# Retention attention and a maxout FFN: two neighbouring weight pieces in one load, and one exponent step moved

## The chip, the cores and the metric

The kernel runs on one core of one Trainium2 chip. Times are device microseconds (us) of one execution, as the median of several runs; a profile is one execution more, recorded by the hardware. The core has five engines that run side by side, each with a queue of its own that is worked off in order: TensorE (PE in the profile, its weight loads PEld), VectorE (DVE), ScalarE (ACT), GpSimd (POOL) and SyncE (SP), which here issues loads and stores. A "q" behind an engine's name means its sequencer, so SPq lines are DMA issues.

## The reference

The program has two parts. The first is causal retention over 8 batches, 8 heads, 576 positions and 64 dimensions a head; the second a maxout feed-forward network over the 4608 rows that come out of it.

```python
scores = scale * np.matmul(q, k.transpose(0, 1, 3, 2))
Dmat = np.where(rel >= 0, gamma[:, None, None] ** rel[None, :, :], 0.0)
attn = np.matmul(scores * Dmat[None, :, :, :], v)          # (B, H, S, D)
x = attn.transpose(0, 2, 1, 3).reshape(B * S, H * D)       # (4608, 512)
h = np.maximum(np.maximum(x @ w1, x @ w2), x @ w3)         # (4608, 768)
return h @ w_out                                           # (4608, 512)
```

The four weights arrive as float64: w1, w2 and w3 are 512 x 768, w_out is 768 x 512.

## The kernel before

**Blocks and tiles.** The 4608 rows are cut into 36 blocks of 128 positions (C), four of which make a tile of 512 (NT). A block's q, k and v are loaded (line 259), q and k are transposed on PE (line 295) and copied out of PSUM by ScalarE into kT and qT (line 296), the scores are taken (line 309), masked by VectorE into st (line 221), and multiplied with v (line 464); what comes from older positions is carried in a state (products at line 423, its use at line 479). The result goes to xT, the FFN's input, with the dimension on the partitions. The FFN's up products of the first tile are at line 934, those of the later tiles at line 909.

**The weights.** They are turned into float32 on the chip, from the bits of the float64. `pieces` lists them in the order of use: for each pair of 128-column blocks of the hidden dimension, and for each of w1, w2, w3, two pieces of 128 columns (512 x 128 numbers, 512 KB as float64); then six pieces of w_out. `load_weights(n)` (lines 596 to 610) takes the next n pieces. Two neighbouring pieces share a tile of the tag "bits". A piece of w1, w2 or w3 is loaded by two DMAs of 256 KB, one for each half of the 128 partitions, because the heads are kept in another order on the partitions; every run in HBM is 128 numbers of 8 bytes, 1 KB. A piece of w_out is one DMA of 512 KB with runs of 4 KB.

**The conversion.** The class `Two` has the steps for a pair of pieces: `exponent` (two ScalarE operations, lines 778 and 779), `fraction` (ScalarE at 785 and 788, VectorE at 786), `whole` (VectorE, 791), `sign` (VectorE, 795), `product` (VectorE, 803), which writes the float32 weights and calls `load_weights(1)` for each piece done. The generator `convert_all` goes through the first three pairs piece by piece and through the others pair by pair; every `yield` in it ends one part, and `convert(n)` runs the next n parts. For the first piece the parts are: exponent, fraction, whole, sign with product; the second piece's follow in the same way.

**The order.** Nothing is scheduled by a planner: the order of the program text is the order in every engine's queue. Lines 1059 to 1107 write out the start by hand: which loads stand in which order on SP's queue, which block's transposes, scores, state and values follow on PE, and where `convert` puts the weights' steps between them. After them the loop over tiles calls `ffn(t)` and the attention of the following tile in turns. Blocks 0 to 3 make the first tile; block CPT - 1 is block 3. `first_ups` starts the up products with the first two pieces of w1, on the columns of blocks 0 to 2, before block 3 is finished.

The lines that the change moves are, in the part before the loop:

```python
    load(2, "kq")
    load_weights(1)
    load(2, "v")
    load(CPT - 1, "kq")
    load_weights(1)
    load(CPT - 1, "v")
    load_weights(2)
    load_weights(2)
    decay(0)
```

`decay(0)` multiplies block 0's v by the keys' decay (line 270; on GpSimd for blocks 0 to 2, on VectorE for block 3).

Of the kernel before, what the change touches and what calls it, by code (L numbers as in the profile page):

```python
# [40 lines left out]
FP32 = mybir.dt.float32  # L41
BF16 = mybir.dt.bfloat16
I32 = mybir.dt.int32
U32 = mybir.dt.uint32
I64 = mybir.dt.int64
AF = mybir.ActivationFunctionType
# [53 lines left out]
def kernel(  # L100
# [14 lines left out]
    nc = tc.nc  # L115
# [30 lines left out]
    def half(j):  # L146
        return slice(D * j, D * (j + 1))
# [97 lines left out]
    def load(g, names="kqv"):  # L245
        if g >= BY_PE and "q" in names and ("q", g) not in raws:
            load_blocks(g, *range(C // 32))
        for n, src in (("k", k), ("q", q), ("v", v)) if g < BY_PE else (("k", k), ("v", v)):
            if n not in names:
                continue  # L250
            bufs = {"k": 3, "q": 2, "v": 4}[n]
            pool, bufs = (raw0, 1) if n != "v" and g < BY_PE and g % (bufs + 1) == bufs else (raw, bufs)
            if n == "v":
                t = vpool.tile([C, H, D], FP32, tag="v", name="vraw")
            else:
                t = pool.tile([C, H, D], FP32, tag=n, name=n + "raw", bufs=bufs)
            raws[n, g] = t
            for row, b, pos, m in spans(g):
                nc.sync.dma_start(t[row:row + m], src[b, :, pos:pos + m, :].rearrange("h p d -> p h d"))  # L259
# [15 lines left out]
    def transposes(g, names="kq"):  # L275
        both = qks.setdefault(g, {})
        if both:
            pass
        elif g >= BY_CHUNKS:
            for n, tag in (("k", "kT"), ("q", "m1")):  # L280
                both[n] = att.tile([P, H, D], FP32, tag=tag, name=n + "T", bufs=2 if n == "k" else 3)
        else:
            both["k"] = att.tile([P, NP, C], FP32, tag="kT", name="kT", bufs=2)
            both["q"] = ppool.tile([P, NP, C], FP32, tag="part", name="qT")
        if g >= BY_PE:
            for n in ("k", "q"):
                soon(partial(nc.vector.transpose, both[n][:].rearrange("a p c -> a (p c)"),
                             raws.pop(("kx" if n == "k" else n, g))[:].rearrange("a x y i -> a (x y i)")))
            return
        for n in names:  # L290
            src = raws["k", g] if n == "k" else raws.pop(("q", g))
            pool, tag = (ps_r, "r") if g >= CPT else (ps_x, "x")
            pt = pool.tile([P, NP, C], FP32, tag=tag, name=n + "t")
            for p in range(NP):
                nc.tensor.transpose(pt[:, p, :], pair(src, p), ident[:C, :C])
            nc.scalar.copy(both[n][:], pt[:])
# [145 lines left out]
    def head(c, n):  # L442

        return NP * c + n
# [151 lines left out]
    def load_weights(n):  # L596
        for _ in range(n):
            if not to_load:
                return
            i, fb = piece = to_load.popleft()  # L600
            if fb % 2 == 0:
                bits[i, fb // 2] = wraw.tile([P, 2, DM], I64, tag="bits", name="bits")
            t = bits[i, fb // 2][:, fb % 2, :]
            if i == "out":
                nc.sync.dma_start(t, moe_w_out[fb * P:(fb + 1) * P, :])
            else:
                heads = WS[i][:, fb * P:(fb + 1) * P].rearrange("(h p) f -> p h f", p=D)
                blocks = t.rearrange("p (n f) -> p n f", f=P)
                for c in range(2):
                    nc.sync.dma_start(blocks[half(c)], heads[:, head(c, 0):head(c, NP)])  # L610

    def seven_forms(order):

# [148 lines left out]
    def convert_all():  # L762

        class Two:
            def __init__(self, n):
                self.i, fb = pieces[2 * n]
                self.fp = fb // 2
                words = bits.pop((self.i, self.fp))[:].rearrange("p e f -> p (e f)")  # L770
                self.high = words.bitcast(I32).rearrange("p (e f two) -> p e f two", e=2, two=2)[:, :, :, 1]
                self.top = words.bitcast(BF16).rearrange("p (e f four) -> p e f four", e=2, four=4)[:, :, :, 3]
                self.low = words.bitcast(U32).rearrange("p (e f two) -> p e f two", e=2, two=2)[:, :, :, 0]
                self.expo = wtmp.tile([P, 2, DM], I32, tag="expo", name="expo")
                self.mant = wtmp.tile([P, 2, DM], FP32, tag="mant", name="mant")

            def exponent(self, e):
                nc.scalar.activation(self.expo[:, e, :].bitcast(FP32), self.top[:, e, :], AF.Abs)
                nc.scalar.activation(self.mant[:, e, :], self.low[:, e, :], AF.Identity, bias=one[:], scale=2.0 ** -52)

            def fraction(self, e):
                expo = self.expo[:, e, :]
                if e != TWO[1]:
                    self.frac = wtmp.tile([P, 2, DM], I32, tag="frac", name="frac", bufs=1)
                nc.scalar.activation(expo, expo, AF.Relu, bias=top[:], scale=-2.0 ** -20)
                nc.vector.tensor_scalar(out=self.frac[:, e, :], in0=self.high[:, e, :], scalar1=0xFFFFF, scalar2=None,
                                        op0=ALU.bitwise_and)
                nc.scalar.activation(expo, expo, AF.Relu, bias=inf[:], scale=-2.0 ** 23)

            def whole(self, e):  # L790
                nc.vector.scalar_tensor_tensor(out=self.mant[:, e, :], in0=self.frac[:, e, :], scalar=2.0 ** -20,
                                               in1=self.mant[:, e, :], op0=ALU.mult, op1=ALU.add)

            def sign(self, e):
                nc.vector.scalar_tensor_tensor(out=self.expo[:, e, :], in0=self.high[:, e, :], scalar=-2 ** 31,
                                               in1=self.expo[:, e, :], op0=ALU.bitwise_and, op1=ALU.bitwise_or)

            def product(self, e):
                if self.i == "out":
                    w = w_out[:, self.fp]  # L800
                else:
                    w = w_up[self.i][:, 2 * self.fp:2 * self.fp + 2, :]
                nc.vector.tensor_tensor(w[:, e, :], self.mant[:, e, :], self.expo[:, e, :].bitcast(FP32), op=ALU.mult)
                for n in range(2)[e]:
                    w_sb[self.i, 2 * self.fp + n] = w[:, n, :]
                    load_weights(1)

        TWO = [slice(0, 1), slice(1, 2)]
        both = slice(0, 2)
        two = Two(0)  # L810
        for e in TWO:
            for step in (two.exponent, two.fraction, two.whole):
                step(e)
                yield
            two.sign(e)
            two.product(e)
            yield
        for n in (1, 2):
            two = Two(n)
            for e in TWO:  # L820
                for step in (two.exponent, two.fraction):
                    step(e)
                    yield
            for e in TWO:
                two.whole(e)
                yield
                two.sign(e)
                two.product(e)
                yield
        two = Two(3)  # L830
        two.exponent(both)
        yield
        two.fraction(both)
        two.whole(both)
        yield
        for n in range(4, len(pieces) // 2 + 1):
            following = Two(n) if n < len(pieces) // 2 else None
            if following:
                following.exponent(both)
            two.sign(both)  # L840
            yield
            two.product(both)
            yield
            if following:
                following.fraction(both)
                yield
                following.whole(both)
                yield
            two = following
# [28 lines left out]
    def convert(n):  # L878
        for _ in range(n):
            next(converting, None)  # L880
# [179 lines left out]
    load(0)  # L1060
    load(1)
    load(2, "kq")
    load_weights(1)
    load(2, "v")
    load(CPT - 1, "kq")
    load_weights(1)
    load(CPT - 1, "v")
    load_weights(2)
    load_weights(2)
    decay(0)  # L1070
# [28 lines left out]
    scores(2)  # L1099
    convert(2)  # L1100
    transposes(CPT - 1, "k")
    state(2)
    values([2], [2], middle=[partial(transposes, CPT - 1, "q")])
    keep(2)
    convert(2)
    scores(CPT - 1)
    decay(CPT - 1)

# [98 lines left out]
```

## Time and profile before

| | |
|---|---|
| median of 3 runs | 738.89 us (738.87 to 738.95) |
| the profiled execution | 738.46 us |
| its span, first to last instruction | 736.7 us |
| PE busy | 731.4 us |
| VectorE busy | 572.3 us |
| ScalarE busy | 354.6 us |
| GpSimd busy | 39.1 us |
| loads of w1, w2, w3 | 36, of 256 KB, 6.2 us to landing (median) |
| loads of w_out | 6, of 512 KB, 5.7 us to landing |
| read from HBM, written | 48.80 MB, 9.44 MB |

The profiled execution is one run by itself; a sum of durations from its rows is made against its own 738.46 us, of which 736.7 are the span. A row of a timeline has the start and the time it took in us, engine, line, operation, out<-in by the program's names, how many, and in brackets the idle time of the engine just before and what ended it. A row of the chain of waits has start, us, and what was last to end there. Matmul times overlap, since matmuls are pipelined; the spacing of their starts tells more than one's own duration. DMA issues have their own rows on SP; the landing is the issue's start and the time to landing.

### The profile page before, as it was taken

What the parts mean: (1) busy time and instruction counts of PE and PEld (TensorE: products, weight loads), DVE (VectorE), ACT (ScalarE), POOL (GpSimd) and SP (SyncE); (2) the same over time, 40 slices, a digit from 0 to 9 for tenths busy, and PEclk for the clock granted to TensorE, in tenths of its full rate; (3) what the DMA queues carried; (4) which work ended last, traced back from release to release, by engine and by line L of the source; (5) the groups of instructions that cost most, each with busy time, mean ns of one, the idle gap of its engine ahead of it and who ended that gap; (6) DMA issues with size and microseconds to landing.
All of it is one profiled execution on the core that took longest, in us unless ns stands there. A gap on an engine that the chain in (4) does not pass through costs nothing.

```text
span 736.7 us, 17316 instructions
## 1 busy us (share of the span) xinstructions
PE 731.4 (99%) x6932; PEld 604.1 (82%) x6932; DVE 572.3 (78%) x1051; ACT 354.6 (48%) x740; POOL 39.1 (5%) x44
## 2 busy tenths in 40 slices
PE   9999999999999999999999999999999999999998
PEld 7654457888888888888888888888888888888887
DVE  5998799999886995689668866887768866893676
ACT  4886915444345525543364425543555245424441
POOL 2000010132000100010000000000100010000000
PEclk9999999999999999999999999999999999999999
DMA  9999554314251415151424243322514150000001
GB/s 222 264 233 247 107 98 115 67 27 91 73 100 27 91 42 105 37 97 32 103 52 79 45 109 60 64 53 64 109 29 88 46 125 6 1 31 28 1 1 57
DMA packets 233264, 59.38 MB, mean 81 GB/s; under 512 B 214496, under 2 KB 231904, under 8 KB 233184
## 3 DMA queue, kind: packets, MB, share of 16 engines
q1 hardware_dynamic: 232208, 58.24, 36.5%
q8 instruction: 54, 0.88, 0.5%
q14 instruction: 26, 0.21, 0.1%
q10 hardware_dynamic: 976, 0.04, 0.1%
HBM read 48.80 MB, written 9.44 MB: 79 GB/s over the span
## 4 chain that ended last, share of the span: by engine, by line
PE 97%; SPq 1%; DMA 1%; issue 0%; ACT 0%; DVE 0%
PE a L909 20%; PE b L909 17%; PE c L909 9%; PE up L934 9%; PE di L755 7%; PE d L909 6%; PE e L909 6%; PE dhc L755 5%; PE deg L755 3%; PE sk L377 3%; PE down L921 3%; PE o L528 2%; PE o L535 2%; PE dfd L755 2%; PE dx L662 1%; SPq L259 1%
## 5 line engine op out<-in xcount | busy, mean ns | idle before, releaser
L897 DVE TENSOR_TENSOR part<-part 128x512 f32<-128x512 f32 x168 | 117.9, 702 | 86.5 <-ACT part L894 83.9
L894 ACT COPY part<-b 128x512 f32<-128x512 f32 x120 | 70.3, 586 | 163.3 <-PE b L909 161.6
L897 DVE TENSOR_TENSOR h<-h,part 128x512 f32<-128x512 f32 x120 | 83.3, 694 | 24.0 <-ACT h L894 20.0
L894 ACT COPY part<-a 128x512 f32<-128x512 f32 x96 | 56.3, 586 | 51.6 <-PE a L909 51.1
L209 ACT ACTIVATE vraw<-vraw,gk 128x64 f32<-128x64 f32 x240 | 76.9, 347 | 6.6 <-DMA vraw<-in_v_dram 6.6
L909 PE MATMUL b<-s,n 128*128 128x256 f32 x288 | 73.9, 379 | 0.0
L934 PE MATMUL up<-xT,w 128*128 128x512 f32 (+2 forms) x160 | 63.5, 553 | 0.0
L909 PEld LDWEIGHTS b<-s,n 128*128 128x128 f32 x288 | 54.7, 190 | 7.4
L394 POOL TENSOR_TENSOR s<-s,gs_of 64x512 f32<-64x512 f32 x23 | 25.0, 1089 | 553.6 <-DVE s L392 476.5
L934 PEld LDWEIGHTS up<-xT,w 128*128 128x128 f32 x160 | 28.6, 190 | 30.1 <-issue 27.0
L909 PE MATMUL c<-xT,w 128*128 128x256 f32 x192 | 51.3, 389 | 0.0
L744 ACT COPY k<-di 128x256 f32<-128x256 f32 x49 | 18.3, 373 | 68.5 <-PE di L755 43.4
L909 PE MATMUL d<-s,w 128*128 128x256 f32 x192 | 49.8, 380 | 0.0
L909 PE MATMUL b<-xT,n 128*128 128x256 f32 x192 | 49.3, 379 | 0.0
L909 PE MATMUL a<-s,w 128*128 128x256 f32 x192 | 49.3, 379 | 0.0
L909 PE MATMUL a<-xT,w 128*128 128x256 f32 x192 | 49.3, 379 | 0.0
L909 PE MATMUL e<-xT,w 128*128 128x256 f32 x192 | 45.4, 379 | 0.0
L909 PE MATMUL a<-xT,n 128*128 128x256 f32 x192 | 45.4, 379 | 0.0
L909 PEld LDWEIGHTS e<-xT,w 128*128 128x128 f32 x192 | 36.5, 190 | 5.4 <-issue 0.5
L909 PEld LDWEIGHTS b<-xT,n 128*128 128x128 f32 x192 | 36.5, 190 | 5.0
L909 PEld LDWEIGHTS a<-s,w 128*128 128x128 f32 x192 | 36.5, 190 | 5.0
L909 PEld LDWEIGHTS a<-xT,w 128*128 128x128 f32 x192 | 36.5, 190 | 5.0
(196 smaller groups left out, 1382.1 us busy)
## 6 DMA issues: line engine op xcount, KB each, us to landing
bits<-in_moe_w_dram SPq DMA_DIRECT2D x36, 256.0 KB, 6.2
kraw<-in_k_dram SPq DMA_DIRECT2D x32, 256.0 KB, 3.1
vraw<-in_v_dram SPq DMA_DIRECT2D x32, 256.0 KB, 3.6
qraw<-in_q_dram SPq DMA_DIRECT2D x240, 32.0 KB, 2.1
kxraw<-in_k_dram SPq DMA_DIRECT2D x240, 32.0 KB, 2.1
out_dram<-osb SPq DMA_DIRECT2D x56, 128.0 KB, 1.7
bits<-in_moe_w_out_dram SPq DMA_DIRECT2D x6, 512.0 KB, 5.7
out_dram<-osb SPq DMA_DIRECT2D x7, 256.0 KB, 2.0
```

The lines of the kernel that those rows point to most:

```text
L209: scaling.popleft()()
L377: nc.tensor.matmul(s[half(c), h, :], lhsT=kT[half(c), h, :], rhs=qT[half(c), h, :], start=True, stop=True)
L394: nc.gpsimd.tensor_tensor(new, new, factor, op=ALU.mult)
L528: nc.tensor.matmul(o[m][half(c), n, u, :], lhsT=vds[g][half(m), h, :], rhs=sts[g][half(m), h, :], start=n == 0 and u == 0, stop=place(g, m ...
L535: nc.tensor.matmul(o[m][half(c), n, u, :], lhsT=stacks[g][half(m), h, :], rhs=qks[g]["q"][half(m), h, :], start=False, stop=True, skip_gro ...
L744: nc.scalar.copy(place, a)
L755: nc.tensor.matmul(banks[chain], lhsT=hidden(h, order, b, late_ones)[:, e], rhs=late["V"][v][:, e], start=begins and e == 0, stop=chain no ...
L894: nc.scalar.copy(of[step], ps[step[0]][:])
L897: nc.vector.tensor_tensor(of[dst], a, b, op=op)
L909: nc.tensor.matmul(ps[chain][:, e, :], lhsT=factor(w, 2 * fp + e), rhs=xS[t][x], start=n == 1 and e == 0, stop=ends, skip_group_check=True)
L921: nc.tensor.matmul(b[:], lhsT=h[:, fb, m * P:(m + 1) * P], rhs=w_sb["out", fb], start=fb == blocks[0], stop=fb == blocks[-1])
L934: nc.tensor.matmul(ps[:, a:b], lhsT=w_sb[i, fb][:, dc * P:(dc + 1) * P], rhs=xT[t][:, dc, a:b], start=dc == 0 and a == 0, stop=dc == NDC - ...
```

## The change

Three things are done together.

- `load_weights` loads the two neighbouring pieces of w1, w2 or w3 with the first of them: two DMAs of 512 KB, one for each half of the partitions, with runs of 256 numbers, 2 KB. The call for the second piece of the pair does nothing. w_out is loaded as before.
- In the tiles of the bits and of what is worked out from them, the two pieces now lie interleaved, as the load brings them: four blocks of 256 columns, in each the 128 of the first piece and the 128 of the second. `of(e, ...)` picks one piece's part where a step works on one alone. `product` writes the float32 weights in their old place.
- At the start, both pieces of w1's first pair are loaded where the first piece was, ahead of block 2's v and block 3's k, q and v; and the second piece's `exponent` runs between the transposes of block 3's k and its q's, where `fraction` stays behind `keep(2)`.

```diff
@@ load_weights
-            t = bits[i, fb // 2][:, fb % 2, :]
+            t = bits[i, fb // 2]
             if i == "out":
-                nc.sync.dma_start(t, moe_w_out[fb * P:(fb + 1) * P, :])
-            else:
-                heads = WS[i][:, fb * P:(fb + 1) * P].rearrange("(h p) f -> p h f", p=D)
-                blocks = t.rearrange("p (n f) -> p n f", f=P)
-                for c in range(2):
-                    nc.sync.dma_start(blocks[half(c)], heads[:, head(c, 0):head(c, NP)])
+                nc.sync.dma_start(t[:, fb % 2, :], moe_w_out[fb * P:(fb + 1) * P, :])
+                continue
+            if fb % 2:
+                continue
+            heads = WS[i][:, fb * P:(fb + 2) * P].rearrange("(h p) f -> p h f", p=D)
+            blocks = t[:].rearrange("p e f -> p (e f)").rearrange("p (n f) -> p n f", f=2 * P)
+            for c in range(2):
+                nc.sync.dma_start(blocks[half(c)], heads[:, head(c, 0):head(c, NP)])
@@ Two
+            def of(self, e, *tiles):
+                if e is both:
+                    return tiles
+                return [t.rearrange("p (n e f) -> p n e f", e=2, f=P)[:, :, e, :] for t in tiles]
+
             def exponent(self, e):
-                nc.scalar.activation(self.expo[:, e, :].bitcast(FP32), self.top[:, e, :], AF.Abs)
-                nc.scalar.activation(self.mant[:, e, :], self.low[:, e, :], AF.Identity, bias=one[:], scale=2.0 ** -52)
+                expo, mant, top, low = self.of(e, self.expo, self.mant, self.top, self.low)
+                nc.scalar.activation(expo.bitcast(FP32), top, AF.Abs)
+                nc.scalar.activation(mant, low, AF.Identity, bias=one[:], scale=2.0 ** -52)
...
             def product(self, e):
+                mant, expo = self.of(e, self.mant, self.expo.bitcast(FP32))
                 if self.i == "out":
                     w = w_out[:, self.fp]
+                    both_of = w.rearrange("p e f -> p (e f)")
                 else:
                     w = w_up[self.i][:, 2 * self.fp:2 * self.fp + 2, :]
-                nc.vector.tensor_tensor(w[:, e, :], self.mant[:, e, :], self.expo[:, e, :].bitcast(FP32), op=ALU.mult)
-                for n in range(2)[e]:
+                    both_of = w.rearrange("p e (n f) -> p n e f", f=P)
+                    if e is both:
+                        mant, expo = (x.rearrange("p (n e f) -> p n e f", e=2, f=P) for x in (mant, expo))
+                    else:
+                        both_of = both_of[:, :, e, :]
+                nc.vector.tensor_tensor(both_of, mant, expo, op=ALU.mult)
+                for n in (0, 1) if e is both else (e,):
                     w_sb[self.i, 2 * self.fp + n] = w[:, n, :]
                     load_weights(1)
@@ the start
     load(2, "kq")
-    load_weights(1)
+    load_weights(2)
     load(2, "v")
-    load(CPT - 1, "kq")
-    load_weights(1)
-    load(CPT - 1, "v")
+    load(CPT - 1, "kqv")
     load_weights(2)
     load_weights(2)
     decay(0)
@@
     scores(2)
     convert(2)
     transposes(CPT - 1, "k")
+    convert(1)
     state(2)
     values([2], [2], middle=[partial(transposes, CPT - 1, "q")])
     keep(2)
-    convert(2)
+    convert(1)
     scores(CPT - 1)
     decay(CPT - 1)
```

`fraction`, `whole` and `sign` are rewritten with `of` in the same way as `exponent`.

More of the change, by code (lines that the diff above doesn't have):

```diff
@@ L770, in __init__ @@
                 words = bits.pop((self.i, self.fp))[:].rearrange("p e f -> p (e f)")
[L771 to L775, printed above, removed]
+                self.high = words.bitcast(I32).rearrange("p (f two) -> p f two", two=2)[:, :, 1]
@@ new lines, in __init__ @@
+                self.top = words.bitcast(BF16).rearrange("p (f four) -> p f four", four=4)[:, :, 3]
+                self.low = words.bitcast(U32).rearrange("p (f two) -> p f two", two=2)[:, :, 0]
+                self.expo = wtmp.tile([P, 2 * DM], I32, tag="expo", name="expo")[:]
+                self.mant = wtmp.tile([P, 2 * DM], FP32, tag="mant", name="mant")[:]
+            def of(self, e, *tiles):
+                if e is both:
+                    return tiles
+                return [t.rearrange("p (n e f) -> p n e f", e=2, f=P)[:, :, e, :] for t in tiles]
@@ L781, in fraction @@
             def fraction(self, e):
-                expo = self.expo[:, e, :]
-                if e != TWO[1]:
-                    self.frac = wtmp.tile([P, 2, DM], I32, tag="frac", name="frac", bufs=1)
+                if e != 1:
+                    self.frac = wtmp.tile([P, 2 * DM], I32, tag="frac", name="frac", bufs=1)[:]
+                expo, frac, high = self.of(e, self.expo, self.frac, self.high)
                 nc.scalar.activation(expo, expo, AF.Relu, bias=top[:], scale=-2.0 ** -20)
-                nc.vector.tensor_scalar(out=self.frac[:, e, :], in0=self.high[:, e, :], scalar1=0xFFFFF, scalar2=None,
-                                        op0=ALU.bitwise_and)
+                nc.vector.tensor_scalar(out=frac, in0=high, scalar1=0xFFFFF, scalar2=None, op0=ALU.bitwise_and)
@@ L788, in fraction @@
                 nc.scalar.activation(expo, expo, AF.Relu, bias=inf[:], scale=-2.0 ** 23)
             def whole(self, e):
-                nc.vector.scalar_tensor_tensor(out=self.mant[:, e, :], in0=self.frac[:, e, :], scalar=2.0 ** -20,
-                                               in1=self.mant[:, e, :], op0=ALU.mult, op1=ALU.add)
+                mant, frac = self.of(e, self.mant, self.frac)
+                nc.vector.scalar_tensor_tensor(out=mant, in0=frac, scalar=2.0 ** -20, in1=mant,
+                                               op0=ALU.mult, op1=ALU.add)
@@ L794, in sign @@
             def sign(self, e):
-                nc.vector.scalar_tensor_tensor(out=self.expo[:, e, :], in0=self.high[:, e, :], scalar=-2 ** 31,
-                                               in1=self.expo[:, e, :], op0=ALU.bitwise_and, op1=ALU.bitwise_or)
+                expo, high = self.of(e, self.expo, self.high)
+                nc.vector.scalar_tensor_tensor(out=expo, in0=high, scalar=-2 ** 31, in1=expo,
+                                               op0=ALU.bitwise_and, op1=ALU.bitwise_or)
@@ L805, in product @@
+                nc.vector.tensor_tensor(both_of, mant, expo, op=ALU.mult)
+                for n in (0, 1) if e is both else (e,):
                     w_sb[self.i, 2 * self.fp + n] = w[:, n, :]
                     load_weights(1)
-        TWO = [slice(0, 1), slice(1, 2)]
-        both = slice(0, 2)
+        TWO, both = (0, 1), "both"
         two = Two(0)
```

## The prediction

> **What bounds the kernel now.** I read the page first, for the share of each engine.
>
> ```profile
> span 736.7 us, 17316 instructions
> PE 731.4 (99%) x6932; PEld 604.1 (82%) x6932; DVE 572.3 (78%) x1051; ACT 354.6 (48%) x740; POOL 39.1 (5%) x44
> ```
>
> TensorE (PE) is busy for 731.4 of 736.7 us, so the change, which alters no matmul, can gain only from the 5.3 us left. Next I read what PE waited for, over the whole span: who is waited for, us in all, times, the longest.
>
> ```profile
> PE warm L176 <- DVE inf L587: 1.1, 1, 1.1
> PE kt L295 <- DMA kraw<-in_k_dram: 0.3, 1, 0.3
> PE o L497 <- ACT first L510: 0.3, 1, 0.3
> PE s L309 <- ACT qT L296: 0.2, 1, 0.2
> PE o L464 <- DVE xT L221: 0.2, 1, 0.2
> ```
>
> The first is the start, before any data. The other four are 1.0 us together; the rest of the 5.3 (some 3.2) lies behind the last matmul. From about 20 us on PE runs without a stop but for one 0.3 us, so whatever delays the start delays the end by as much. Third, the chain of waits in the first 30 us (start us, us, what):
>
> ```profile
> 9.61 0.60 SPq L259
> 10.21 0.04 issue
> 10.26 5.82 DMA kraw<-in_k_dram
> 16.08 0.14 issue
> 16.21 0.63 PE kt L295 x4
> 16.84 0.61 PE kv L423 x16
> 17.46 0.88 PE o L464 x16
> 18.33 0.60 PE qt L295 x4
> 18.93 0.02 issue
> 18.95 0.59 ACT qT L296
> 19.55 0.04 issue
> 19.59 1.16 PE s L309 x16
> 20.75 2.78 PE up L934 x8
> ```
>
> The landing of block 3's k at 16.08 sets the time from which PE never stops. That wait ends last in the one stage that has slack, and its loads stand in one queue. So, fourth, that queue's order in time:
>
> ```profile
> 7.97 1.59 SPq L610 DMA_DIRECT2D bits<-in_moe_w_dram  x2
> 9.61 0.60 SPq L259 DMA_DIRECT2D vraw<-in_v_dram  x1
> 10.26 0.58 SPq L259 DMA_DIRECT2D kraw<-in_k_dram  x1
> 10.96 2.55 SPq L259 DMA_DIRECT2D qraw<-in_q_dram  x1
> 13.55 2.27 SPq L610 DMA_DIRECT2D bits<-in_moe_w_dram  x2
> ```
>
> Block 3's k (10.26) is issued behind the first piece of w1 (two loads of 256 KB) and block 2's v; the second piece goes out at 13.55, behind block 3's k and q. The DMA engines are full here (the page's first four slices read 9), so an earlier load delays all behind it.
>
> **The change, part by part.**
>
> *Second piece ahead of block 3's k.* Both pieces now go out at 7.97 and 8.96 as two loads of 512 KB, so 512 KB more (0.524 MB) stand ahead of v 2, k 3 and q 3. Issue times and times to landing give landings: q 2 at 6.92 + 4.3 = 11.2, the first piece's halves at 7.97 + 4.9 = 12.9 and 8.96 + 5.0 = 14.0, v 2 at 9.61 + 5.6 = 15.2, k 3 at 16.1. The piece thus took 14.0 - 11.2 = 2.7 us of the queue (later pieces take less; there some DMA engines trail the others). What 2 KB packets do no row shows for loads; the nearest are two long weight stretches, 39 to 46 us (1 KB packets) and 61.8 to 63 us (w_out, 4 KB packets):
>
> ```profile
> DMA packets 1851, 1.75 MB, mean 250 GB/s; under 512 B 182, under 2 KB 1849, under 8 KB 1849
> DMA packets 136, 0.49 MB, mean 407 GB/s; under 512 B 17, under 2 KB 17, under 8 KB 136
> ```
>
> From 20 to 27 us 1 KB packets reach 278 GB/s. Bounds: at 407 GB/s both pieces together take 1.049/407 = 2.6 us, what one takes now, so k 3 is late by 0 (-0.1). If the doubled piece costs twice the present 2.7 us, it is late by 2.7. Between: 0.524 MB more at 250 GB/s is 2.1 us, at 278 1.9. I take 2.1, because the 1 KB row has what the changed load keeps: each load fills only 64 partitions and its rows lie 6 KB apart in HBM. w_out's load fills 128 partitions from whole rows, so its 407 may belong to that and not to the packet.
>
> [...]
>
> Who waits: PE's queue is in order, and the transposes of k 3 (16.21, idle 0.30 before them) already wait, so the delay passes in full. Behind them stand kv, o, qt, the scores and the first up product, no one with another cover. v 2 is as late, and POOL's decay of it (15.31, 1.04 us) ends at 16.35 + 2.1, still ahead of kv (16.77 + 2.1). ScalarE's first exponent starts on the landing (14.07) and its four operations end at 16.77, ahead of the kT copy at 16.88: both shift alike. VectorE's first fraction (14.08, 0.43) waits on the same landing, now near 16.1, and block 1's xT (0.76) and block 2's st (1.29) are behind it: st ends near 18.6 where PE needs it at 17.29 + 2.1. After that whole, sign and product (0.7 each) end near 20.6; the first up needs them at 20.68 + 2.1. **Sum: +2.1.**
>
> *Exponent 2 ahead of the q copy.* Two ScalarE operations (680 and 750 ns, overlapping: 19.44 to 20.77), no DMA, move past one ScalarE instruction, the qT copy; PE and VectorE work that they pass is on other queues. ScalarE now idles 1.49 us before that copy (kT ends at 17.47, qT starts at 18.95). From 17.37 they end at 18.70, so they fit with 0.25 to spare. Their data lands with the first piece's. **0**; if they ran 0.3 us longer, or their data came late, the qT copy and PE's scores would be late by what exceeds 0.25. What they free at 20.68 is no gain: VectorE is full from 19.55 to 31 and the second product ends at 25.20, set by VectorE's row, while PE comes to it at 25.55.
>
> *Order of bits in the tile.* For the first six pieces an operation on one piece walks four runs of 128 instead of 512 in line: six instructions each of seven kinds, by 0.42 to 0.76 us now. No row shows such a walk for them; the nearest, xT at L221, writes runs of 128 and takes 0.38 us per 256 elements, against 0.42 for a plain 256 at L433. So 0, between -0.04 and +0.1 each; the second product's four VectorE steps have 0.35 us of slack before PE. The joint pieces keep 1024 elements an instruction; only the last write is in another order. **0.**
>
> *Later loads.* 36 loads of 256 KB become 18 of 512, issued no later than now. Loads of k, q, v behind them are pushed by at most one piece, 1 to 2 us; block 4's k is needed at 40.32 and lands near 31. v 3 moves ahead in the queue but not in bytes: about 20, needed by VectorE at 22.55 + 2.1. Faster packets there gain nothing, as PE does not wait. **0.**
>
> The sum against the profiled execution (738.46 us; its span 736.7 and 1.8 around it) is 740.6. It lies 0.43 under the median 738.89, so on the median **741.0 us**, +0.28%. A measurement of this kernel can tell about 0.2%, 1.5 us, from no change.
>
> **The rivals.**
>
> 1. *2 KB packets run clearly faster than 1 KB.* For it: 407 against 250 GB/s. Against: partitions and rows differ too. Halfway, 330 GB/s, the two pieces take 3.2 us against 2.7, plus the trailing of the slowest engine: +0.3 to +1.4, say 739.9. Within 0.2%.
> 2. *Not slower.* One mechanism: the pieces reach the 4 KB rate. It decides at 1.049 MB in 2.7 us, 388 GB/s: from there k 3 is no later, and at best the 0.3 us wait at 16.08 goes. 738.6 to 738.9.
> 3. *The exponent blocks the q copy.* If the interleaved halves are held to overlap, exponent 2 waits for the first product (20.6 with the shift) and the qT copy starts near 22.0 and not 21.05: +0.9 more, 742. Against it: PE's up product reads columns 0 to 383 of xT from 25.55 while VectorE writes 384 to 511 of each of its rows from 25.66, with no wait between.
> 4. *PE's clock falls in the longer wait.* The granted clock reads 1.00 throughout, but the first twelve matmuls, 128 wide, took 2.93 us and four like them at 40.48 took 0.44, so a cold PE runs at about half speed; the slow spell, 1.1 to 4.7, cost 1.8 us, the price again: 743. The longest later wait so far is 0.3 us; this one would be 2.4.
> 5. *Faster by over 0.2%.* It would need more than the 1.0 us of waits that there are.
>
> [...]
>
> **How the numbers follow.** Forecast (k 3 late by 1.6 to 2.7, 740.5 to 741.6): 0.55. Rival 1: 0.22. Rival 2: 0.06. Rivals 3 and 4 on top of the forecast: 0.14. Rival 5: 0.03. Slower: 0.55 + 0.14 = 0.69; same 0.28; faster 0.03. The range reaches down into rival 1 to 739.2 and up to rival 3's and part of rival 4's, 742.3; outside stay rivals 2 and 5 and the ends, under 0.2.
>
> **What would show it.** Right: the wait of kt for k 3 grows from 0.3 to about 2.4 us, that load lands near 18.2, the first up starts near 22.8, PE's other waits stay, and the exponent lies between the kT and qT copies. Wrong: k 3 landing before 17.5 (rival 1), weight stretches of 2 KB packets at 350 GB/s or more, PE waiting over 0.5 us for qT (rival 3), or four 128-wide transposes taking 0.9 us after the wait (rival 4).

## The result and the profile after

The kernel after takes 743.34 us in the median of six runs (741.10 to 744.47), the kernel before 738.88 us in six runs beside them (738.74 to 739.09). The ratio is 1.0058, with an interval of 1.0044 to 1.0072: slower by 4.5 us. The forecast was 741.0 with a range of 739.2 to 742.3. The direction was right and the size was not; the time lies outside the range.

The profiled execution of after took 743.69 us. Its page, the first part and the row of the weights' loads in the sixth:

```profile
span 741.9 us, 17280 instructions
PE 732.6 (99%) x6932; PEld 604.9 (82%) x6932; DVE 572.4 (77%) x1051; ACT 354.1 (48%) x740; POOL 39.0 (5%) x44
...
bits<-in_moe_w_dram SPq DMA_DIRECT2D x18, 512.0 KB, 8.7
```

The span grew by 5.2 us (741.9 against 736.7). The work is what it was: VectorE and ScalarE differ by 0.1 and 0.5 us. PE is busy for 1.2 us more, with the same 6932 matmuls. So there is idle time and, to be explained, slower matmuls. What PE waited for in after, over the span (us in all, times, the longest):

```profile
PE kt L295 <- DMA kraw<-in_k_dram: 3.5, 1, 3.5
PE warm L176 <- DVE inf L587: 1.1, 1, 1.1
PE qt L295 <- DMA qraw<-in_q_dram: 0.6, 1, 0.6
PE o L497 <- ACT first L510: 0.3, 1, 0.3
```

The wait for block 3's k grew from 0.3 to 3.5 us; 2.4 was forecast. The 0.6 us are for block 0's q at 5.2 us, a load that stands ahead of all weights; the profiles of the other kernels have 0 to 0.5 us there. The chain of waits of after shows what lay behind it (start us, us, what):

```profile
10.19 0.60 SPq L259
10.79 0.04 issue
10.84 8.63 DMA kraw<-in_k_dram
19.47 0.14 issue
19.60 0.63 PE kt L295 x4
20.23 0.61 PE kv L423 x16
20.85 1.35 PE o L464 x16
22.20 1.05 PE qt L295 x4
23.24 1.06 PE o L479 x16
24.30 1.21 PE s L309 x16
25.51 2.78 PE up L949 x8
```

It is the same chain as before, with three differences. The k load takes 8.63 us to land where it took 5.82. From the row of 20.85 on PE's own steps are longer: 1.35 and 1.05 us for o and qt, which took 0.88 and 0.60 before. And between qt and the scores stands PE's own o (1.06) where before had ScalarE's qT copy (0.59): PE is now the slower of the two. From the start of kt to the first up it is 5.91 us now (25.51 - 19.60) and was 4.54 (20.75 - 16.21).

That is the clock. PE by stretches of 3.41 us in after, with the granted clock in the column PEclk (the columns are given by the second line):

```profile
core 0: us, PE busy (x) PEld busy (x) DVE busy (x) ACT busy (x) POOL busy (x), PEclk, DMA share, GB/s
14.27:17.69 3.42, 1.87 (x36) 1.40 (x32) 0.00 (x0) 0.00 (x0) 0.00 (x0) 1.00 1.14 205
17.69:21.10 3.41, 1.50 (x28) 1.36 (x30) 2.97 (x7) 2.95 (x5) 1.61 (x2) 1.00 0.86 191
21.10:24.51 3.41, 3.41 (x34) 2.42 (x32) 1.38 (x3) 2.62 (x5) 0.00 (x0) 0.50 1.04 245
24.51:27.92 3.41, 3.41 (x24) 2.24 (x24) 3.38 (x8) 1.62 (x3) 0.37 (x1) 1.00 1.06 221
```

From 21.10 to 24.51 us TensorE had half its clock (0.50), behind the wait, and PE was full in that time; so every matmul there was paid for.

The 5.2 us of span are then: 0.22 by which PE came later to the end of block 2's scores (they start at 14.97 us here, at 14.75 in before, and between 14.64 and 15.40 over all fourteen profiles), 3.17 more of waiting for k 3, 1.37 more from kt to the first up at the lower clock, 0.29 near 599 us, where one group of kv products starts later, and 0.15 behind the last matmul. Four of the experiments' profiles shift at those kv products too, by 0.28 to 0.54 us, the others and before's don't; the cause stays open. Between the first up and that place PE's products stand a constant 4.75 to 4.77 us later. Nothing is given back.

Why k 3 is late is in SP's queue of after, in time:

```profile
8.49 1.66 SPq L612 DMA_DIRECT2D bits<-in_moe_w_dram  x2
10.19 0.60 SPq L259 DMA_DIRECT2D vraw<-in_v_dram  x1
10.84 0.58 SPq L259 DMA_DIRECT2D kraw<-in_k_dram  x1
11.54 6.05 SPq L259 DMA_DIRECT2D qraw<-in_q_dram  x1
```

The order is the one that was forecast. Issue times and times to landing give the landings:

| landing at, us | before | after |
|---|---|---|
| q 2 | 11.25 | 11.55 |
| first halves, second halves of the first load | 12.82, 13.99 | 14.69, 18.03 |
| v 2 | 15.24 | 18.63 |
| k 3 | 16.08 | 19.47 |

The joint load occupies the queue for 18.03 - 11.55 = 6.5 us, and one piece took 13.99 - 11.25 = 2.7. Twice the bytes took 2.4 times as long, and k 3 is late by 3.39, more than the 2.7 that had been the upper bound. The pair's own landing is a rough measure: the five profiles that load w1's first pair in this shape (after, and e3, e4, e9 and e10 of the experiments below) put it 4.7 to 6.5 us behind q 2, and after's is the longest. What repeats is k 3: it lands 7.3 to 7.9 us behind q 2 in these five and 4.8 in before. In the long weight stretches it is the same. First before from 20 to 27 us:

```profile
DMA packets 2023, 1.95 MB, mean 278 GB/s; under 512 B 123, under 2 KB 2023, under 8 KB 2023
```

and after from 24 to 34 us, where the packets are 2 KB:

```profile
DMA packets 1150, 2.24 MB, mean 224 GB/s; under 512 B 65, under 2 KB 65, under 8 KB 1149
```

So there are half as many packets for the bytes, and they move slower: 224 GB/s against 278, or the 250 of before's later stretch.

Last, the moved exponent, on ScalarE of after (rows of the timeline):

```profile
20.72 0.57 ACT L296 COPY kT<-kt 128x512 f32<-128x512 f32 x1
21.18 0.67 ACT L786 ACTIVATE expo<-bits 128x512 f32<-128x512 bf16 x1
21.76 0.76 ACT L787 ACTIVATE mant<-bits,one 128x512 f32<-128x512 uint32 x1
23.28 0.58 ACT L296 COPY qT<-qt 128x512 f32<-128x512 f32 x1 [0.77 <-PE qt L295]
```

It lies between the two copies and ends 0.77 us before PE's qt releases the second; it blocks nothing, and it does not wait for the first product.

### The profile page after: what moved, and what is told of

Same layout as the page of the kernel before. It is cut to its first block, busy times and chain, and to the rows that moved or that the text cites. A ratio compares the mean times of both kernels' runs of the same rounds, so it can differ in the third digit from the quotient of the medians.

```text
span 741.9 us, 17280 instructions
## 1 busy us (share of the span) xinstructions
PE 732.6 (99%) x6932; PEld 604.9 (82%) x6932; DVE 572.4 (77%) x1051; ACT 354.1 (48%) x740; POOL 39.0 (5%) x44
## 4 chain that ended last, share of the span: by engine, by line
PE 97%; SPq 1%; DMA 1%; issue 0%; DVE 0%; ACT 0%
PE a L924 20%; PE b L924 17%; PE c L924 9%; PE up L949 8%; PE di L757 7%; PE d L924 6%; PE e L924 6%; PE dhc L757 5%; PE deg L757 3%; PE sk L377 3%; PE down L936 3%; PE o L528 2%; PE o L535 2%; PE dfd L757 2%; PE dx L664 1%; DMA kraw<-in_k_dram 1%
## 5 line engine op out<-in xcount | busy, mean ns | idle before, releaser
L924 PE MATMUL d<-s,w 128*128 128x256 f32 x192 | 49.8, 380 | 0.0
```

The source lines that it names most:

```text
L924: nc.tensor.matmul(ps[chain][:, e, :], lhsT=factor(w, 2 * fp + e), rhs=xS[t][x], start=n == 1 and e == 0, stop=ends, skip_group_check=True)
```

## The experiments

The theory that I formed from the two traces, theory A in the expectations: the time is set by when k 3 lands, that by the bytes ahead of it at the rate that a load into 64 partitions has (250 to 278 GB/s in before, 224 with the joint load), and by what the half clock behind the long wait costs. Against it stand that it is the 2 KB packet itself, that it is the moved exponent or the interleaved tiles, that the later loads cost by themselves, and that the clock costs nothing. Ratios are against before, run beside each experiment; its medians there were 738.95 (e1 to e4), 739.07 (e5 to e8) and one execution of 738.36 (e9 to e12).

### e1: the order alone

Before, with both pieces of the first pair ahead of block 2's v, as two times two loads of 256 KB with 1 KB packets:

```diff
     load(2, "kq")
-    load_weights(1)
+    load_weights(2)
     load(2, "v")
-    load(CPT - 1, "kq")
-    load_weights(1)
-    load(CPT - 1, "v")
+    load(CPT - 1, "kqv")
```

> The kernel before with one edit: both pieces of w1's first pair ahead of block 2's v and block 3's k, as four loads of 256 KB with 1 KB packets; conversion order as before. Theory A (bytes ahead of block 3's k, and 1 KB packets at 250 to 278 GB/s): k 3 lands 1.9 to 2.3 us later than the 16.1 of before, PE waits some 2.4 us for it, the clock holds, 740.8 to 741.2. Theory B (any further pair ahead of k 3 costs what the changed kernel lost, packets do not matter): k 3 near 19.5, PE waits 3.5 us, clock 0.997, 743.3. Rival C (the order costs nothing, the loss is in the 2 KB loads): 738.9.

Measured: 741.79 us (740.84 to 742.49, six runs), ratio 1.0038 (1.0026 to 1.0051). The wait for k 3 in its profile:

```profile
PE kt L295 <- DMA kraw<-in_k_dram: 2.3, 1, 2.3
```

k 3 lands at 18.45 us, 2.4 later than in before, and the first up is later by as much. This is the forecast's term for 512 KB more ahead of k 3 (2.1 at 250 GB/s) and nearly its size. The four loads land 4.8 us behind q 2 (12.29 to 17.12), so a piece costs 2.4 here. Two further profiles of this kernel (e11, e12) have k 3 at 19.03 and 18.06; counted from q 2 it lands 6.2 to 7.0 us later in the three. The runs fall into two groups: 740.84, 740.94 and 741.41 us at a mean clock of 1.0, and 742.17, 742.35 and 742.49 at 0.997 or 0.998. The profiled one is of the first group: the clock held through a wait of 2.3 us.

### e2: joint loads into all partitions

After, with each 512 KB load spread over 128 partitions, same bytes, same 2 KB packets:

```diff
-            heads = WS[i][:, fb * P:(fb + 2) * P].rearrange("(h p) f -> p h f", p=D)
+            rows = WS[i][:, fb * P:(fb + 2) * P].rearrange("(n p) f -> p n f", p=P)
...
-                nc.sync.dma_start(blocks[half(c)], heads[:, head(c, 0):head(c, NP)])
+                nc.sync.dma_start(blocks[:, 2 * c:2 * c + 2], rows[:, 2 * c:2 * c + 2])
```

> The changed kernel, but each of a pair's two 512 KB loads fills all 128 partitions with two of the four column blocks (rows of w1, w2, w3 in their natural order, so the heads are taken in a wrong order and the output is not the reference's); still 2 KB packets, rows 6 KB apart. Theory A (a load that fills 64 partitions is held to about half the rate, 217 to 230 GB/s, whatever its packets): the weight-only stretches rise to 380 GB/s or more, the first pair takes about 2.8 us of the queue and not 6.5, k 3 lands before 17.2, PE waits under 1.3 us, clock 1.00, 738.8 to 740.0. Theory B (2 KB packets or rows 6 KB apart are slow in HBM): stretches stay at 220 to 250 GB/s, k 3 near 19.5, 743.3.

Measured: 740.02 us (739.50 to 742.09, ten runs), ratio 1.0016 (1.0007 to 1.0026). The wait is 0.7 us. The joint load lands 2.6 us behind q 2 (11.62 to 14.21) instead of 6.5. A weight stretch of it, 20 to 26 us:

```profile
DMA packets 1232, 2.39 MB, mean 399 GB/s; under 512 B 70, under 2 KB 70, under 8 KB 1231
```

So it isn't the packet: 2 KB packets move 399 GB/s into 128 partitions and 224 into 64. Even packets of 256 B move faster than that over all partitions: in after, k 3 and q 3, 256 KB each in such packets, land 0.84 and 0.89 us behind the load ahead of them, 312 and 295 GB/s. Most of the loss goes with the 128 partitions. What is left, k 3 at 16.93 (0.85 later than before), comes behind v 2, which lands at 15.11, as early as before; why k 3 then takes 1.8 us more and not 0.8 isn't settled (in e7 it is 1.7).

### e3: PE kept busy while it waits

After, with 16 matmuls of the identity ahead of block 3's transposes:

```diff
+    busy = ps_x.tile([P, P], FP32, tag="x", name="busy")
+    for _ in range(16):
+        nc.tensor.matmul(busy[:], lhsT=ident[:], rhs=ident[:], start=True, stop=True)
     transposes(CPT - 1, "k")
```

> The changed kernel with 16 matmuls of the identity with itself (about 0.21 us each, 3.4 us in all) put on PE just ahead of the transposes of block 3's k, where it now waits 3.5 us. Theory A (1.4 us of the loss is PE's clock, which halves after the wait): granted clock 1.00 throughout, the values of block 2 take 0.9 us and not 1.35, 741.8 to 742.2 and less spread over the runs than 741.1 to 744.5. Rival (the slow matmuls behind the wait are slow for another reason, as data that comes late): 743.3 or a little more.

Measured: 742.45 us (742.24 to 742.93, four runs), ratio 1.0046 (1.0031 to 1.0061); the mean clock is 0.999 to 1.0 in all four. PE in its timeline, from 16 to 26 us (start, us, line, operation, tiles; the 16 matmuls leave 32 records, and the last row is cut off at 26):

```profile
16.22 3.84 PE L1116 MATMUL busy<-ident 128*128 128x128 f32 x32
19.90 0.60 PE L295 MATMUL kt<-ident,kraw 128*128 128x128 f32 x4
20.43 0.69 PE L423 MATMUL kv<-vd,kraw 128*64 128x64 f32 x16
20.94 1.05 PE L464 MATMUL o<-st,vd 128*64 128x128 f32 x16
...
24.34 1.88 PE L949 MATMUL up<-xT,w 128*128 128x384 f32 x5
```

k 3 lands at 19.72 here, 0.25 later than in after's profile, and the first up still starts at 24.34, where the timeline of after has it at 25.44. From kt to the first up it is 4.44 us again, with nothing changed but that PE had work to do in the wait. So the half clock costs 1.4 us in that stretch, and without it the median is 0.9 us lower (743.34 to 742.45). In this profile, the longest of the four runs, a further 0.7 us goes from 97 us on, where PE waits 0.4 us for VectorE; no other profile has that wait. The times of this kernel spread over 0.7 us, those of after over 3.4.

### e4: the exponent moved back

```diff
     transposes(CPT - 1, "k")
-    convert(1)
     state(2)
...
     keep(2)
-    convert(1)
+    convert(2)
```

> The changed kernel with the second piece's exponent back behind the state of block 2 (both of its parts there, as before). Theory A (the moved exponent is idle ScalarE time): 743.3 within 0.5, the clock as in the changed kernel. Rival (the exponent ahead of the q copy holds PE's scores up): up to 1 us less, 742.3, with PE's wait for qT shorter.

Measured: 743.66 us (742.64 to 744.46, four runs), ratio 1.0061 (1.0046 to 1.0076); after has 1.0058. So the move shows no cost and no gain.

### e5: only the later pairs joint

After, with the first pair of w1 as in before (two pieces of 1 KB packets, the old order, the exponent in its old place), and 2 KB packets from the second pair on:

```diff
+            if (i, fb // 2) == (0, 0):
+                heads = WS[i][:, fb * P:(fb + 1) * P].rearrange("(h p) f -> p h f", p=D)
+                blocks = t[:].rearrange("p e f -> p (e f)").rearrange("p (n e f) -> p n e f", e=2, f=P)[:, :, fb]
+                for c in range(2):
+                    nc.sync.dma_start(blocks[half(c)], heads[:, head(c, 0):head(c, NP)])
+                continue
...
```

> The changed kernel, but w1's first pair is loaded and converted as before: two pieces by themselves with 1 KB packets, the second behind block 3's k and q, its exponent behind the state of block 2. Left of the change are the interleaved tiles and the 17 later loads of 512 KB with 2 KB packets. Theory A (all of the loss is made ahead of block 3's k): k 3 near 16.1, PE waits 0.3 us for it, the clock holds, 738.9 within 0.3, although the weight stretches run at 220 to 230 GB/s. Rival (the later loads or the interleaved steps cost by themselves): 739.5 or more, with new waits of PE behind 25 us.

Measured: 740.67 us (738.99 to 742.39, ten runs), ratio 1.0021 (1.0011 to 1.0031). Theory A had the time of before, and that falls: the later loads cost 1.6 us by themselves (0.8 to 2.3 by the interval). In its profile (741.13 us, one of the longer) PE's timeline shows where, in two places:

```profile
30.97 2.41 PE L955 MATMUL up<-xT,w 128*128 128x512 f32 x5 [0.30 <-DVE w L825]
...
54.47 0.63 PE L295 MATMUL kt<-ident,kraw 128*128 128x128 f32 x4 [0.47 <-DMA kraw<-in_k_dram]
55.30 0.63 PE L295 MATMUL qt<-ident,qraw 128*128 128x128 f32 x4 [0.21 <-DMA qraw<-in_q_dram]
```

The weights of the second pair are late for the up products at 30.97, and block 5's k and q come late at 54 us, because slower weight loads stand ahead of them in the queue (block 5's k lands at 54.3, in before at 49.8). The up products are 0.5 us later than in before at first, where k 3 lands at 16.57, and 2.1 us later behind the second place. After has none of these waits: its PE runs some 5 us later, and what is late for e5's PE is there in time for that one. The costs of the first pair and of the later ones therefore don't add.

### e6: the halves in turns

After, with the 512 KB of each half cut into two loads of 256 KB, and the halves taken in turns; 2 KB packets:

```diff
-            for c in range(2):
-                nc.sync.dma_start(blocks[half(c)], heads[:, head(c, 0):head(c, NP)])
+            for n in (0, 2):
+                for c in range(2):
+                    nc.sync.dma_start(blocks[half(c), n:n + 2], heads[:, head(c, n):head(c, n + 2)])
```

> The changed kernel with each half's 512 KB load cut in two of 256 KB, the halves of the partitions in turns; packets stay 2 KB, bytes and order of the pieces stay. Theory A (the rate hangs on how long a stretch the DMA engines spend on one half of the partitions): the weight stretches return to the 250 to 278 GB/s of before, the first pair takes 4 to 5 us and not 6.5, k 3 near 18.2, 740.8 to 742.4 with the clock falling in some runs only. Rival (2 KB packets into 64 partitions are slow by themselves): 220 to 230 GB/s, k 3 near 19.5, 743.3.

Measured: 741.99 us (740.67 to 742.72, six runs), ratio 1.0037 (1.0025 to 1.0048), that is e1's, with 2 KB packets where e1 has 1 KB. k 3 lands at 18.22, the wait is 1.8 us. The stretch from 24 to 34 us:

```profile
DMA packets 3111, 2.47 MB, mean 247 GB/s; under 512 B 2149, under 2 KB 2149, under 8 KB 3111
```

Two thirds of these packets are small ones of k and q; the six weight loads that land from 26.51 to 32.65 us move 256 GB/s, which is e1's rate in such a stretch (254). k 3 lands 6.9 us behind q 2, within e1's 6.2 to 7.0 and below the 7.3 to 7.9 of the joint loads. The runs stand again in two groups, 740.67 to 741.44 at a clock of 1.0 and 742.54 to 742.72 at 0.998, as e1's do, where e3, which has the joint loads and holds its clock, takes 742.24 to 742.93. So what the joint load lost against two pieces, some 1 us by these groups, is not the packet's size: it comes back when a load takes 256 KB and the halves alternate, instead of 512 KB into one half at a stretch. Which of the two does it, the smaller load or the turns, no run separates; 512 KB loads are not slow as such, since e2's move 399 GB/s.

### e7: before, with its pieces over all partitions

Before, with each 256 KB load over 128 partitions, 1 KB packets (the edit of e2, on one piece).

> The kernel before (1 KB packets, its order of loads) with each piece's two loads filling all 128 partitions, two of the four column blocks each (natural rows, so the output is not the reference's). Theory A (64 or 128 partitions is what sets the rate): 1 KB packets too reach 340 to 390 GB/s where before had 250 to 278; k 3 lands up to 1 us earlier, PE's wait of 0.3 for it goes, 738.5 to 738.9. Rival (1 KB packets are slow as such, only packets of 2 KB and more gain from 128 partitions): 250 to 278 GB/s, 738.9.

Measured: 738.97 us (738.61 to 740.93, ten runs), ratio 1.0001 (0.9991 to 1.0010). k 3 lands at 15.60 and PE doesn't wait for it. In the weight stretches most loads of 256 KB land 0.63 to 0.77 us behind the one ahead of them (single ones 1.2 to 1.7), at the common 0.68 us 385 GB/s, so 1 KB packets too move that fast over all partitions. And it gains nothing that can be measured: PE is busy for all of the time behind the start, and the wait that goes is the 0.3 us that there was. So a faster load has next to nothing to gain here, and no version that beats before follows from these runs.

### e8, e9 and e10: which partitions, which rows

The rate of a load into 64 partitions could come from which 64 they are or from the rows that the DMA engines read. e8 sends 512 KB to partitions 32 to 95 and the other halves as 256 KB each to 0 to 31 and 96 to 127:

```diff
+            nc.sync.dma_start(blocks[32:96], heads[:, 0:NP])
             for c in range(2):
-                nc.sync.dma_start(blocks[half(c)], heads[:, head(c, 0):head(c, NP)])
+                nc.sync.dma_start(blocks[96 * c:96 * c + 32], heads[32 * c:32 * c + 32, NP:2 * NP])
```

> The changed kernel with a pair loaded as 512 KB into partitions 32 to 95, then 256 KB into 0 to 31 and 256 KB into 96 to 127 (wrong heads, output not the reference's). [...] Rival (any 64 partitions are slow): the 512 KB load takes 2.2 to 2.4 us as in the changed kernel, the others 1.1 each.

Measured: 743.65 us (741.62 to 744.47, three runs), ratio 1.0056 (1.0039 to 1.0072). In the weight stretches the 512 KB into the middle land 2.3 to 2.6 us behind the load ahead of them (30.36 - 28.03 = 2.33), some 225 GB/s. So these 64 partitions are as slow as the halves are in after (224 GB/s).

e9 gives each partition four consecutive rows of HBM, and e10 every other row, by the source alone:

```diff
-            heads = WS[i][:, fb * P:(fb + 2) * P].rearrange("(h p) f -> p h f", p=D)
+            rows = WS[i][:, fb * P:(fb + 2) * P].rearrange("(c p n) f -> c p n f", c=2, n=NP)
...
-                nc.sync.dma_start(blocks[half(c)], heads[:, head(c, 0):head(c, NP)])
+                nc.sync.dma_start(blocks[half(c)], rows[c])
```

(e10 has "(n p c) f -> c p n f".)

> The changed kernel with the same two 512 KB loads into the halves of the partitions, 2 KB packets, but each partition takes four rows that follow one another in HBM (wrong rows, output not the reference's). [...] Theory B (64 partitions are slow whatever is read): 220 to 230 GB/s, k 3 near 19.5, 742 to 744.

> [...] Theory A (HBM rows): 380 GB/s or more, k 3 before 17.2, 739 to 740. Theory B (64 partitions): 220 to 230 GB/s, k 3 near 19.5, 742 to 744. If only one of the two runs is fast, the distance of the rows decides, and which.

Measured, one execution each: 743.27 us with a wait of 2.7 us and 222 GB/s from 24 to 34 us, and 743.44 us with 2.9 us and 221 GB/s. Neither choice of rows is faster.

### e11 and e12: the order alone, twice more

The kernel of e1 again, to see one of its slower executions in a profile.

> The kernel before with both 1 KB pieces ahead of block 3's k, once more, for the clock: its profile had a wait of 2.3 us at a clock of 1.00, while three of its six runs had 0.997 or 0.998 and 1.4 us more. Theory A (the wait's length decides): with a wait up to 2.3 us the clock holds and the run takes 740.8 to 741.4; with 2.5 or more the slices behind it read 0.5 to 0.9 and it takes 742.2 to 742.5. Rival (the clock falls by chance, whatever the wait): a fall with a wait of 2.3 or less.

> The same kernel for a second profile, with the same expectations: a wait up to 2.3 us and 740.8 to 741.4 at a clock of 1.00, or 2.5 us and more with a fall of the clock and 742.2 to 742.5; rival: a fall with a wait of 2.3 us or less.

Measured: 742.98 us with a wait of 2.83 us, and 741.75 with 2.39; in both the clock fell. e12 by stretches, the columns as above, and below it e1's stretch with its wait, behind which the clock held, and e11's, behind which it fell:

```profile
14.24:17.65 3.41, 1.56 (x32) 1.20 (x26) 2.57 (x6) 1.97 (x3) 0.41 (x1) 1.00 0.94 196
17.65:21.06 3.41, 2.86 (x30) 2.56 (x32) 2.50 (x3) 0.59 (x1) 1.99 (x2) 0.50 1.01 252
...
16.79:20.20 3.41, 1.62 (x30) 1.45 (x32) 3.38 (x5) 0.66 (x2) 2.52 (x2) 1.00 0.88 205
...
15.84:19.25 3.41, 0.58 (x11) 0.42 (x8) 3.04 (x6) 0.97 (x2) 1.03 (x1) 1.00 0.81 179
```

In e12 the clock fell at 17.65 us, while PE was still waiting (it went on at 18.20); in after it fell at 21.10, 1.5 us after PE had gone on. And e12's wait of 2.39 us is hardly longer than the 2.29 through which the clock held in e1. What these profiles tell of the difference is in the last section.

## Why the prediction was right and wrong

**Right.** PE is the bound, and what delays its start delays the end by as much: the up products stand a constant 4.75 us later. The place was right (k 3 behind the first weights in SP's queue, then kt), and so was the mechanism in e1, +2.4 us for 512 KB more ahead of it. The exponent's move shows no effect (e4); at a full clock, in e3, it ends 0.23 us before the qT copy can start, and 0.25 was forecast. Rival 3 is false, and the interleaved tiles cost nothing that VectorE's or ScalarE's busy time would show: e6, which has them, runs as e1, which has not. Rivals 1 and 2, faster packets, are false: 224 GB/s, not 330 or 388. Rival 5 had nothing to take, and e7 shows how little a faster load brings.

**The term that was mis-sized: k 3 late by 2.1, at most 2.7.** It measured 3.4 in after's profile, 0.3 of it because q 2 itself came later. Counted from q 2, k 3 lands 4.8 us later in before; the forecast made that 6.9, at most 7.5. With the second piece ahead of it in loads of 256 KB it is 6.2 to 7.0 (e1, e6, e11, e12), near the forecast; with the joint loads it is 7.3 to 7.9. The step took the rate of 1 KB packets, 250 GB/s, as what 2 KB packets into 64 partitions would have at worst; the upper bound was twice the present 2.7 us. It left no room for a joint load that is slower by the byte. It was, 224 GB/s against 250 to 278, because it puts 512 KB into one half of the partitions at a stretch (e6, e2). The forecast did see that each load fills only 64 partitions, and used it only against a gain. It was a resource that before's trace did not show alone, and so the bound should have reached to a loss as well: with one half at a time at 407/2 = 204 GB/s, half of the 4 KB row that filled all partitions, the pair takes 1.049/204 = 5.1 us, an estimate from that row; 6.5 were measured.

**The rival that was given too small a chance: the clock.** Rivals 3 and 4 had 0.14 together, with a price of 1.8 us for the clock. The step that failed is to give the rival so little beside "this one would be 2.4 us": the longest later wait in before was 0.3 us, so that the clock would hold through a longer one was not shown. The wait came out at 3.5 us; but e12 shows a fall at 2.39, so even at the size that I forecast it was about an even chance (the kernel of e1: five of its eight executions). The price was 1.37 us, by after's chain, and e3 shows that it is the clock. The sign that the forecast named for this rival, transposes of 0.9 us right behind the wait, did not come: kt took 0.63 us as before, and the clock fell 1.5 us later, under o and qt.

**The zero that was only a zero under cover: later loads.** "PE does not wait there" holds in after, since its PE runs 5 us later. By itself the slower rate of the later loads costs 1.6 us (e5), in two places that the forecast didn't go through with a slower load: the second pair's weights at 31 us and block 5's k and q at 54. Nor are the loads behind pushed by "1 to 2 us": block 4's k lands at 30.9 us in before and at 37.8 in after, still ahead of the 45.1 at which PE comes to it there.

In after's profile the order of the loads costs 1.8 of the 3.4 us (6.65 us from q 2 to k 3 in the mean of e1, e6, e11 and e12, against 4.83), the joint loads 1.3 more (7.92), the later q 2 0.3; the clock, which falls in most executions of after and not in all (its mean is 0.995 to 0.998 in five of the six and 0.999 in the one of 741.10 us), costs 1.4. Together 4.8, and the first up was 4.76 later.

## What to carry to other kernels

Where PE has no slack, count what stands in the queue ahead of the last load that it waits for, in bytes at the rate that this very shape of load has: two loads made one did not move the same bytes at the same rate here, where each fills only half of the partitions (224 GB/s against 250 to 278). Price a longer wait of PE twice, once as the wait (3.17 us in after) and once as the clock that may fall behind it (1.37). And a zero that another term's delay covers is no zero: say what it costs if that delay is smaller.

## What the runs showed of the hardware

**Half of the partitions, 221 to 278 GB/s against 385 to 399.** Weight stretches moved, by packet and partitions:

| load | GB/s |
|---|---|
| 1 KB, 64 partitions, halves alternate every 256 KB (before in two stretches, e1) | 278, 250, 254 |
| 2 KB, 64 partitions, halves alternate every 512 KB (after, e9, e10) | 224, 222, 221 |
| 2 KB, 64 partitions, halves alternate every 256 KB (e6; the second from its weight landings) | 247, 256 |
| 2 KB, 128 partitions (e2) | 399 |
| 1 KB, 128 partitions (e7, from its landings) | 385 |

The packet's size makes no difference that these rows show; the partitions of a load do. As far as e8 (three executions, one profile) and e9 and e10 (one each) tell, it is neither which 64 they are nor which rows they read. What in the DMA path it is stays open.

**When the clock fell.** In the seven profiles in which it fell on the way (after, e4, e8 to e12), the half clock lasted 3.41 us each time. After's trace has the clock's first record at 4.03 us and the fall of 21.10 us 17.07 behind it, five times 3.41; one more fall, at the end of the trace, is 216 times 3.41 behind that record. In before the only fall is at the end too, 215 times 3.41 behind the first record at 4.66 us. With that the waits can be laid over stretches of 3.41 us, and PE's idle time taken in each: its length less PE's busy time. In after, e11 and e12 the stretches are counted back from the fall; e1 has none, and where its stretch begins is my estimate.

| kernel | stretch, us | PE idle in it, us | the clock after it |
|---|---|---|---|
| after | 14.27 to 17.69 | 1.55 | held |
| e1 | 16.79 to 20.20 | 1.79 | held |
| e12 | 14.24 to 17.65 | 1.85 | fell |
| after | 17.69 to 21.10 | 1.91 | fell |
| e11 | 15.84 to 19.25 | 2.83 | fell |

The other four profiles with a fall have 2.33 to 2.95 us of idle time in the stretch ahead of it (e4, e8, e9, e10). The clock held behind e8's stretch before that, with 1.39, and e6's wait of 1.83 us brought no fall. So in these rows it held behind up to 1.79 us of idle time and fell behind 1.85 and more. That a border lies between the two, and that the place of a wait on these stretches counts beside its length, is an estimate from these few rows and not shown: a border in the wait's length alone, between e1's 2.29 us and e12's 2.39, would agree with them too. With either one, a wait near the border could give one kernel the two groups of times that e1 has: 741 us at a mean clock of 1.0, and 742.3 at 0.997 or 0.998. The idle times are read from profiles in which the ends of matmuls are modelled; no run was made to test the border by itself.
